# The last two blocks of an expert kernel: second-layer products alternated, adds per 128 tokens, state rows stored in three transfers

## The chip, the cores and the metric

The kernel runs on one core of one Trainium2 chip. The metric is the time on the device in microseconds; for each kernel it is the median of several executions. One more execution is recorded by the hardware profiler, and all views shown here come from it. In them PE is the matmul engine, PEld its weight loads, DVE the vector engine, ACT the scalar engine, and SP the engine that issues most of the stores. hps, A, E and Bseed are tiles in the matmul engine's accumulation memory (PSUM), a bank each: 128 partitions by 512 numbers of 32 bits.

## The reference

An attention between tokens and a small state comes first, and then a mixture of eight experts with a balanced routing. Cut to what matters:

```python
# attention: x (8, 8, 512, 64), state (8, 8, 32, 64), for each batch and head
xread = softmax(scale * x @ state.T) @ state
sread = softmax(scale * state @ x.T) @ x
rows = concat([xread, sread], axis=2)          # 512 + 32 rows per batch
x = rows.transpose(0, 2, 1, 3).reshape(8 * 544, 512)

# routing: P = exp(x @ w_gate), then 8 rounds of row and column normalisation
for e in range(8):
    h = np.maximum(x @ w1[e], 0.0)             # first layer: 512 -> 1024
    ye = h @ w2[e]                             # second layer: 1024 -> 512
    out += P[:, e:e + 1] * ye
```

The result has 4352 rows of 512 numbers: for each of the 8 batches 512 rows of tokens and then 32 rows of state.

## The kernel before

**Blocks.** The 4352 rows are worked on in nine blocks: blocks 0 to 7 are the 512 token rows of a batch each, and block 8 is the 8 x 32 = 256 state rows of all batches together. Expert 0 is done together with the attention, in an order that a planner at build time makes out of costs and due times (`issue`). Experts 1 to 7 follow in a plain loop (line 918) over the list `work`, expert after expert and block after block; that loop and the two functions that it steps are all that the change touches, and the order there is the order in which the program is written out.

**First layer** (`layer1`, line 246). For each of eight groups of 128 hidden units: matmuls into one of four `hps` banks (line 239; two matmuls of 512 columns for a token block, four of 256 for the state block), and a ReLU on ACT into the tile `Hm` (line 258). After each four groups, DVE makes four sums and differences of quarters of `Hm` (lines 264 to 267) into `sm` and `Hm`. `Hm` and `sm` come from the pool `hidden`, which holds two of each.

**Second layer** (`layer2`, line 270). The rows of a block are taken as two halves ("row 0" and "row 1"), the hidden units as two halves and the output columns as two halves of 256 (`DH`). The 2 x 2 x 2 product of these is made with seven products instead of eight, from the sums in `sm` and differences of weights in `T`. A product has `nk` parts of 128 tokens, two in a token block and one in the state block, and a part is four matmuls of 256 columns (line 285). Both parts of a product lie in the same bank. There are three banks per block: `A`, `E` and one of the two lasting `Bseed` tiles, which are used in turn. After the first product, ACT copies `A` into `Bseed` (line 310), on which later products accumulate:

```python
product(A, h(0, 0), w2h[:, :NJ, :DH], True)
nc.scalar.copy(out=Bb[:, :nk], in_=A[:, :nk])
product(Eb, s(0), T[:, 0], True);  add(Eb, 1, 1)
product(Bb, s(1), T[:, 1]);        add(Bb, 0, 1)
product(A, h(1, 0), w2h[:, NJ:, :DH]); add(A, 0, 0)
product(Bb, h(0, 1), T[:, 2]);     add(Bb, 1, 1)
product(Eb, s(2), w2h[:, NJ:, DH:]); add(Eb, 0, 1)
product(Bb, h(1, 1), T[:, 3]);     add(Bb, 1, 0)
```

`add(src, row, col)` is a DVE instruction for each 128 tokens (line 299): it takes 256 columns from the bank, multiplies them by the token's weight in `Pmat` and adds them into `acc`, the 4352 x 512 result in on-chip memory. All parts of a product are made before its adds are written out.

**Order.** Both layers are generators. Each step of the loop takes one product of the current block's second layer and then some groups of the next block's first layer, (0, 0, 1, 2, 2, 2, 1) of them after the seven products and the rest behind. So PE alternates between the two layers, with the second layer of one block beside the first layer of the next. For the very last block, block 8 of expert 7, there is no next block.

**Stores.** In expert 7, after a block's last product, SP issues the block's stores: for a token block four of 128 rows (256 KB, line 332), for the state block eight of 32 rows (64 KB, line 335), one for each batch.

Of the kernel before, what the change touches and what calls it, by code (L numbers as in the profile page):

```python
# [9 lines left out]
FP32 = mybir.dt.float32  # L10
FP16 = mybir.dt.float16
AX_X = mybir.AxisListType.X
ALU = mybir.AluOpType
# [74 lines left out]
def kernel(  # L88
# [9 lines left out]
    nc = tc.nc  # L98

    B, H, S, D = x.shape  # L100
    Ns = state.shape[2]
    Dm, E = moe_w_gate.shape
    F = moe_w1.shape[2]
    SB = S + Ns
# [8 lines left out]
    NJ = NFB // 2  # L113
    DH = Dm // 2
# [13 lines left out]
    def bank(shape, dtype, name, tag="bank"):  # L128
        return pools[tag].tile(shape, dtype, name=name, tag=tag)
# [3 lines left out]
    acc = persist.tile([128, NTB, Dm], FP32, name="acc")  # L133
# [15 lines left out]
    w2r = moe_w2.rearrange("e (fb p) d -> e p fb d", p=128)  # L149

    outx = [out[b * SB:b * SB + S, :].rearrange("(p sc) d -> p sc d", sc=NSC) for b in range(B)]
    outs = [out[b * SB + S:(b + 1) * SB, :] for b in range(B)]

    mw = ctx.enter_context(tc.tile_pool(name="moe_w", bufs=2))
    gsb = ctx.enter_context(tc.tile_pool(name="gate_sb", bufs=2))
# [85 lines left out]
    vt = {}  # L241
    ring = ["bank"]
    hid = {}
    seeds = []

    def layer1(e, bi):

        t0, tn = blocks[bi]
        th = tn // 2
        Hm = hpool.tile([128, 2, NJ, S], FP16, name="Hm", tag="Hm")  # L250
        sm = hpool.tile([128, 3, NJ, S // 2], FP16, name="sm", tag="sm")
        hid[(e, bi)] = (Hm, sm)
        for j in range(NJ):
            for i in range(2):
                fb = i * NJ + j
                hps = bank([128, S], FP32, "hps", "h")
                hidden_ps(e, bi, fb, hps[:, :tn])
                nc.scalar.activation(out=Hm[:, i, j, :tn], in_=hps[:, :tn], func=AF.Relu)  # L258
                if j % 2 and i:
                    jj = ds(j - 1, 2)  # L260
                    a11, a21 = Hm[:, 0, jj, :th], Hm[:, 0, jj, th:tn]
                    a12, a22 = Hm[:, 1, jj, :th], Hm[:, 1, jj, th:tn]
                    s1, s2, s4 = (sm[:, k, jj, :th] for k in range(3))
                    nc.vector.tensor_add(s1, a21, a22)  # L264
                    nc.vector.tensor_sub(a21, a11, a21)  # L265
                    nc.vector.tensor_sub(s2, s1, a11)  # L266
                    nc.vector.tensor_sub(s4, a12, s2)  # L267
                yield

    def layer2(e, bi, n):  # L270
        t0, tn = blocks[bi]
        nk = tn // 256
        th = tn // 2
        Hm, sm = hid.pop((e, bi))
        w2h, T = w16[e][1], tsum[e]
        tb = t0 // 128
        p = Pmat[:, :, e:e + 1]
        A = bank([128, 2, DH], FP32, "A", "A")
        Eb = bank([128, 2, DH], FP32, "E", "E")
        Bb = seeds[n % 2]  # L280

        def product(dst, lhs, rhs, first=False):
            for c in range(nk):
                for j in range(NJ):
                    nc.tensor.matmul(dst[:, c], lhs(j, c), rhs[:, j],  # L285
                                     start=first and c == 0 and j == 0, stop=(j == NJ - 1),
                                     skip_group_check=True)

        def h(i, half):
            return lambda j, c: Hm[:, i, j, ds(half * th + c * 128, 128)]  # L290

        def s(k):
            return lambda j, c: sm[:, k, j, ds(c * 128, 128)]

        def add(src, row, col):
            for c in range(nk):
                k = tb + row * nk + c
                dst = acc[:, k, ds(col * DH, DH)]
                nc.vector.scalar_tensor_tensor(out=dst, in0=src[:, c], scalar=p[:, k], in1=dst,  # L299
                                               op0=ALU.mult, op1=ALU.add)  # L300

        if e == 1:
            for k in range(tb, tb + 2 * nk):
                if k % 2:
                    nc.scalar.mul(acc[:, k, :], acc[:, k, :], Pmat[:, k, 0:1])
                else:
                    nc.vector.tensor_scalar(out=acc[:, k, :], in0=acc[:, k, :],
                                            scalar1=Pmat[:, k, 0:1], scalar2=None, op0=ALU.mult)
        product(A, h(0, 0), w2h[:, :NJ, :DH], True)
        nc.scalar.copy(out=Bb[:, :nk], in_=A[:, :nk])  # L310
        yield
        product(Eb, s(0), T[:, 0], True)
        add(Eb, 1, 1)
        yield
        product(Bb, s(1), T[:, 1])
        add(Bb, 0, 1)
        yield
        product(A, h(1, 0), w2h[:, NJ:, :DH])
        add(A, 0, 0)
        yield  # L320
        product(Bb, h(0, 1), T[:, 2])
        add(Bb, 1, 1)
        yield
        product(Eb, s(2), w2h[:, NJ:, DH:])
        add(Eb, 0, 1)
        yield
        product(Bb, h(1, 1), T[:, 3])
        add(Bb, 1, 0)
        if e == E - 1:
            for k in range(2 * nk):  # L330
                if bi < B:
                    nc.sync.dma_start(out=outx[bi][:, k, :], in_=acc[:, tb + k, :])
                else:
                    for i in range(128 // Ns):
                        nc.sync.dma_start(out=outs[k * (128 // Ns) + i],
                                          in_=acc[ds(i * Ns, Ns), tb + k, :])
        yield


# [43 lines left out]
    for q in range(NQ):  # L383
        for par in range(2):
            nc.gpsimd.tensor_copy(
                out=pick[:, q, par].rearrange("p (a i n) -> p a i n", i=2, n=Ns)[:, :, par ^ q],
                in_=identh.rearrange("p (a i n) -> p a i n", i=2, n=Ns)[:, :, par])
# [3 lines left out]
    for q in range(NQ):  # L391
        def load(q=q):
# [4 lines left out]
                           lambda eng, q=q: copy(eng, st16[:, q], st_st.tile.rearrange("p (q b d) -> p q b d", q=NQ, b=B)[:, q]),  # L397
                           [dma((0, q), 300, load, [], [] if q else [st_st])], [], [st_st]))
    wgd = dma((0, 2), 16, lambda: nc.sync.dma_start(
        out=wg_st, in_=moe_w_gate.rearrange("(kc p) e -> p kc e", p=128)))  # L400
# [32 lines left out]
    for b in range(B):  # L433
        for g in range(2):
# [13 lines left out]
            d = dma((0 if b < 1 else 3.2 if b < 2 else due_x(2 * b - 2), b, 0), 512, load, takes=[st])  # L448
# [249 lines left out]
    def tile_of(tag, shape):  # L698
# [3 lines left out]
    c = sk({"DVE": (0.36, 0.48)}, lambda: nc.vector.reduce_max(  # L702
        out=tile_of("lmx", [128, 1]), in_=logits.rearrange("p t e -> p (t e)"), axis=AX_X), gates)
    mT = psum([1, 128], FP32, "mT_ps")
    c = sk({"PE": (0.11, 0.35)}, lambda: nc.tensor.transpose(mT.tile, sm_["lmx"], ident32), [c], takes=[mT])
    c = sk({"DVE": (0.25, 0.40)}, lambda: nc.vector.tensor_reduce(
        out=tile_of("gm", [1, 1]), in_=mT.tile, op=ALU.max, axis=AX_X, negate=True), [c], uses=[mT])
    gb = psum([128, 1], FP32, "gm_ps")
    c = sk({"PE": (0.18, 0.45)}, lambda: nc.tensor.matmul(gb.tile, ones128[0:1, :], sm_["gm"]), [c], takes=[gb])
    c = sk({"DVE": (0.12, 0.25)}, lambda: nc.vector.tensor_copy(out=tile_of("nm", [128, 1]), in_=gb.tile),  # L710
           [c], uses=[gb])
    c = sk({"ACT": (0.40, 0.60)}, lambda: nc.scalar.activation(
        out=Pmat, in_=logits, func=AF.Exp, bias=sm_["nm"]), [c])
    for it in range(8):
# [10 lines left out]
        def colnorm(csb=csb):  # L725
# [7 lines left out]
        c = sk({"DVE": (2.10, 2.25)}, rownorm, [c])  # L733
        c = sk({"PE": (0.25, 0.60)}, lambda csb=csb: nc.tensor.matmul(csb.tile, ones128, sm_["cpart"]),
               [c], takes=[csb])
        c = sk({"DVE": (0.75, 0.90)}, colnorm, [c], uses=[csb])
# [50 lines left out]
    for bi in range(len(blocks)):  # L787
        t0, tn = blocks[bi]
# [5 lines left out]
        for fb in range(NFB):  # L794
            ps = psum([128, 512], FP32, "hps")
            h = slot(mh, 10, [128, 512], FP16, "hT")
# [10 lines left out]
        for tk in range(tn // 128):  # L807
            yps = psum([128, Dm], FP32, "yps")
            last = None
            for half in range(2):  # L810
                def mul(_, tk=tk, half=half, yps=yps, hT=hT):
                    w2h = wslots[0][1].tile
                    for fb in range(half * NJ, half * NJ + NJ):
# [4 lines left out]
                last = op((due_e(bi) + 13.5 * (0.4 + 0.075 * (2 * tk + half)),), {"PE": (0.87, 1.04)}, mul,  # L818
                          [h_ready[fb] for fb in fbs] + w2_ready(0)[2 * half:2 * half + 2] + [last],
                          [] if half else [yps], [hT[fb] for fb in fbs] + ([yps] if half else []))  # L820
# [32 lines left out]
    for bi in range(2):  # L853
        t0, tn = blocks[bi]
        th = tn // 2
# [50 lines left out]
    n = 0  # L906
# [8 lines left out]
                wload.pop(0)  # L915

    work = [(e, bi) for e in range(1, E) for bi in range(len(blocks))]
    for i, (e, bi) in enumerate(work):
        if bi == 1 and e + 1 < E:
            wload.append(load_w(e + 1, (nc.scalar,)))  # L920
        l2 = layer2(e, bi, i)
        l1 = layer1(*work[i + 1]) if i + 1 < len(work) and work[i + 1] not in hid else iter(())
        for k in range(7):
            next(l2)
            step()
            if k == 0 and i + 2 < len(work) and work[i + 2] not in vt:
                project(*work[i + 2])
            for _ in range((0, 0, 1, 2, 2, 2, 1)[k]):
                next(l1, None)
                step()  # L930
        for part in (l1, l2):
            for _ in part:
                pass
        if bi == len(blocks) - 3:
            for _ in (x for w in wload for x in w):
                pass
            wload.clear()


# [28 lines left out]
```

## Time and profile before

| | us |
|---|---|
| median of 3 runs | 782.14 |
| lowest and highest of them | 781.5 and 782.41 |
| profiled execution, its own time | 783.01 |
| span of the profile, from the first to the last instruction | 781.2 |
| PE busy in the span | 755.6 (97%) |
| DVE busy | 635.9 (81%) |
| ACT busy | 518.6 (66%) |
| last matmul ends | 775.2 |
| last add ends | 775.7 |

The profiled execution is 0.9 us above the median, and 1.8 us of it lie outside the span. A row of the chain in order of time gives a start, a duration and what the chain goes through there; a piece called "issue" is the time in which the next engine has not yet begun. A row of the timeline gives start, duration, engine, line, operation, what is written from what, how many instructions are merged, and in brackets the idle time ahead and what ended it. A row for stretches of time gives for each engine its busy time and, in brackets, the instructions that begin there, then the clock granted to PE, the share of the DMA engines, and GB/s.

### The profile page before, as it was taken

Reading aid. Unit: us, or ns where it says so; the run is one execution under the profiler, and the core shown is the slowest. Engines: PE = TensorE matmul, PEld = TensorE weight load, DVE = VectorE, ACT = ScalarE, POOL = GpSimd, SP = SyncE. Lnnn points to the kernel's source line nnn. Section 1 sums busy time; section 2 is a strip of 40 time slices with the busy share of each in tenths; the row PEclk is TensorE's granted clock in tenths of the full one; section 3 lists DMA queues with packets and bytes.
Section 4 is the critical chain, followed back from the end, with each engine's and each line's share of the span. In section 5 each row is a group of like instructions: output and inputs, shape, how many; then the busy total and the mean of one; then the engine's idle time right before and its main releaser. Section 6 shows DMA issues by size and latency. Waiting matters only on the chain.

```text
span 781.2 us, 16249 instructions
## 1 busy us (share of the span) xinstructions
PE 755.6 (97%) x6497; PEld 507.7 (65%) x6497; DVE 635.9 (81%) x1572; ACT 518.6 (66%) x1011; POOL 61.3 (8%) x114
## 2 busy tenths in 40 slices
PE   4799999999999999999999999999999999999996
PEld 3355444566667767766677667766667666766675
DVE  5788878968997888778887888878887888878885
ACT  5676766757767766676666666676657666576662
POOL 3546110010001000000001000000001000000000
PEclk9999999999999999999999999999999999999999
DMA  9996300060006000150006000060005100012223
GB/s 282 304 224 114 50 1 1 1 109 1 1 1 109 2 1 2 16 94 2 1 1 102 9 1 1 3 107 3 1 1 86 25 1 1 2 53 91 91 100 127
DMA packets 43772, 41.43 MB, mean 53 GB/s; under 512 B 18864, under 2 KB 34224, under 8 KB 43696
## 3 DMA queue, kind: packets, MB, share of 16 engines
q0 software_dynamic: 11200, 14.68, 11.6%
q1 hardware_dynamic: 31456, 25.45, 11.4%
q8 instruction: 51, 0.84, 0.5%
q10 hardware_dynamic: 1040, 0.26, 0.2%
q14 instruction: 25, 0.20, 0.1%
HBM read 42.48 MB, written 8.91 MB: 66 GB/s over the span
## 4 chain that ended last, share of the span: by engine, by line
PE 67%; DVE 3%; ACT 1%; issue 0%
PE hps L239 24%; PE Bseed L285 17%; PE E L285 12%; PE A L285 11%; PE v_ps L224 3%; DVE acc L299 1%; DVE sm L264 1%; ACT Hm L258 1%; DVE Hm L265 0%; DVE sm L267 0%; DVE sm L266 0%; DVE T L182 0%; ACT Bseed L310 0%
## 5 line engine op out<-in xcount | busy, mean ns | idle before, releaser
L258 ACT ACTIVATE Hm<-hps 128x512 f16<-128x512 f32 (+1 forms) x488 | 261.6, 572 | 181.8 <-PE hps L239 166.7
L285 PEld LDWEIGHTS <-Hm 128*128 128x128 f16 x1904 | 186.3, 98 | 69.2 <-issue 1.4
L239 PE MATMUL hps<-aT,V 128*128 128x512 f16 x864 | 230.5, 379 | 0.0
L299 DVE SCALAR_TENSOR_TENSOR acc<-Bseed,Pmat,acc 128x256 f32<-128x256 f32 x357 | 156.9, 479 | 56.9 <-PE Bseed L285 54.0
L285 PEld LDWEIGHTS <-sm 128*128 128x128 f16 x1428 | 134.4, 98 | 53.1 <-DVE sm L264 24.4
L285 PE MATMUL Bseed<-T,Hm 128*128 128x256 f16 x952 | 124.5, 273 | 0.7 <-DVE acc L299 0.4
L285 PE MATMUL A<-w2h,Hm 128*128 128x256 f16 x952 | 124.5, 273 | 0.0
L239 PEld LDWEIGHTS <-V 128*128 128x128 f16 x864 | 84.5, 98 | 44.4
L299 DVE SCALAR_TENSOR_TENSOR acc<-E,Pmat,acc 128x256 f32<-128x256 f32 x238 | 104.3, 477 | 9.2 <-PE E L285 5.3
L228 ACT CAST V<-v_ps 128x512 f16<-128x512 f32 x216 | 111.2, 609 | 0.0
L814 PE MATMUL yps<-w2h,hT 128*128 128x512 f16 x272 | 67.3, 383 | 0.0
L285 PE MATMUL E<-T,sm 128*128 128x256 f16 x476 | 64.4, 274 | 0.7
L264 DVE TENSOR_TENSOR sm<-Hm 128x512 f16<-128x512 f16 (+1 forms) x122 | 49.8, 408 | 18.6 <-ACT Hm L258 17.8
L299 DVE SCALAR_TENSOR_TENSOR acc<-A,Pmat,acc 128x256 f32<-128x256 f32 x119 | 52.4, 479 | 15.4 <-PE A L285 15.3
L285 PE MATMUL Bseed<-T,sm 128*128 128x256 f16 x476 | 62.3, 273 | 0.4 <-ACT Bseed L310 0.4
L285 PE MATMUL E<-w2h,sm 128*128 128x256 f16 x476 | 62.3, 273 | 0.0
L265 DVE TENSOR_TENSOR Hm<-Hm 128x512 f16<-128x512 f16 (+1 forms) x122 | 50.0, 410 | 4.2
L267 DVE TENSOR_TENSOR sm<-Hm,sm 128x512 f16<-128x512 f16 (+1 forms) x122 | 50.0, 409 | 4.2
L266 DVE TENSOR_TENSOR sm<-sm,Hm 128x512 f16<-128x512 f16 (+1 forms) x122 | 49.1, 402 | 0.0
L310 ACT COPY Bseed<-A 128x512 f32<-128x512 f32 (+1 forms) x63 | 34.5, 548 | 19.9 <-PE A L285 19.3
L164 POOL DMA_DIRECT2D w1h<-in_moe_w_dram x12 | 8.5, 713 | 457.8 <-PE hps L239 406.4
L814 PEld LDWEIGHTS <-hT 128*128 128x128 f16 x272 | 24.4, 99 | 27.0 <-issue 4.0
(117 smaller groups left out, 589.5 us busy)
## 6 DMA issues: line engine op xcount, KB each, us to landing
stage<-in_x_dram SPq DMA_DIRECT2D x16, 512.0 KB, 6.0
out_dram<-acc SPq DMA_DIRECT2D x32, 256.0 KB, 3.0
w1h<-in_moe_w_dram POOLq DMA_DIRECT2D x14, 512.0 KB, 5.8
w2h<-in_moe_w_dram POOLq DMA_DIRECT2D x14, 512.0 KB, 7.8
stage<-in_moe_w_dram SPq DMA_DIRECT2D x8, 512.0 KB, 5.7
out_dram<-acc SPq DMA_DIRECT2D x8, 64.0 KB, 1.7
stage<-in_state_dram ACTq DMA_DIRECT2D x1, 256.0 KB, 4.9
stage<-in_state_dram SPq DMA_DIRECT2D x1, 256.0 KB, 4.6
```

The lines of the kernel that those rows point to most:

```text
L224: nc.tensor.matmul(ps[q][ds(j * Ns, Ns), :], bdT[ds(r, 64), bi, q, ds(j * Ns, Ns)], w1h[ds(r, 64), 2 * q + j // 2, cols], tile_position=(r ...
L228: nc.scalar.copy(out=V[:, q, cols], in_=ps[q])
L239: nc.tensor.matmul(out, lhs, rhs, start=(k == 0), stop=(k == len(terms) - 1))
L258: nc.scalar.activation(out=Hm[:, i, j, :tn], in_=hps[:, :tn], func=AF.Relu)
L264: nc.vector.tensor_add(s1, a21, a22)
L265: nc.vector.tensor_sub(a21, a11, a21)
L266: nc.vector.tensor_sub(s2, s1, a11)
L267: nc.vector.tensor_sub(s4, a12, s2)
L285: nc.tensor.matmul(dst[:, c], lhs(j, c), rhs[:, j], start=first and c == 0 and j == 0, stop=(j == NJ - 1), skip_group_check=True)
L299: nc.vector.scalar_tensor_tensor(out=dst, in0=src[:, c], scalar=p[:, k], in1=dst, op0=ALU.mult, op1=ALU.add)
L310: nc.scalar.copy(out=Bb[:, :nk], in_=A[:, :nk])
L814: nc.tensor.matmul(yps.tile, hT[fb].tile[:, ds(tk * 128, 128)], w2h[:, fb, :], start=(fb == 0), stop=(fb == NFB - 1))
```

## The change

The last two entries of `work`, blocks 7 and 8 of expert 7, are taken out of the loop. Both their first layers are done during the second layer of block 6, with 0, 2, 3, 3, 3, 3, 2 groups after its seven products. The hidden units of block 8 get tiles of their own, `Hl` and `sl`, from a new pool. Then the two second layers are stepped in turn: two products of block 7, then one of block 8 and one of block 7 alternately, then the last two of block 8. Block 8 takes its `A` and `E` tiles from the four `hps` banks. In block 7 (`split=True`) each 128 tokens' add is written out directly behind their four matmuls, ahead of the matmuls of the next 128 tokens.

The stores of expert 7 are split by row: row 0 leaves after the sixth product, row 1 after the seventh. For token blocks they are the same transfers, on SP. The state block is stored by ACT in three transfers, each over four batches: columns 256 to 511 of row 1 (128 KB) after the fifth product, row 0 whole (256 KB) after the sixth, and columns 0 to 255 of row 1 (128 KB) after the seventh.

```diff
-    outs = [out[b * SB + S:(b + 1) * SB, :] for b in range(B)]
+    outs = out.rearrange("(b s) d -> b s d", b=B)
...
-        Hm = hpool.tile([128, 2, NJ, S], FP16, name="Hm", tag="Hm")
-        sm = hpool.tile([128, 3, NJ, S // 2], FP16, name="sm", tag="sm")
+        if (e, bi) == work[-1]:
+            Hm = lpool.tile([128, 2, NJ, tn], FP16, name="Hl")
+            sm = lpool.tile([128, 3, NJ, th], FP16, name="sl")
+        else:
+            Hm = hpool.tile([128, 2, NJ, S], FP16, name="Hm", tag="Hm")
+            sm = hpool.tile([128, 3, NJ, S // 2], FP16, name="sm", tag="sm")
...
-    def layer2(e, bi, n):
+    def layer2(e, bi, n, AE=("A", "E"), split=False):
...
-        A = bank([128, 2, DH], FP32, "A", "A")
-        Eb = bank([128, 2, DH], FP32, "E", "E")
+        A = bank([128, 2, DH], FP32, "A", AE[0])
+        Eb = bank([128, 2, DH], FP32, "E", AE[1])
...
+        def product(dst, lhs, rhs, row, col, first=False):
+            for c in range(nk):
+                mul(dst, lhs, rhs, c, first)
+                if split:
+                    add(dst, row, col, c)
+            for c in range(0 if split else nk):
+                add(dst, row, col, c)
+
+        def store(row, cols=slice(0, Dm)):
+            for c in range(nk if e == E - 1 else 0):
+                k = row * nk + c
+                if bi < B:
+                    nc.sync.dma_start(out=outx[bi][:, k, :], in_=acc[:, tb + k, :])
+                else:
+                    nc.scalar.dma_start(out=outs[ds(k * (128 // Ns), 128 // Ns), S:, cols],
+                                        in_=acc[:, tb + k, cols])
...
+        product(Bb, h(0, 1), T[:, 2], 1, 1)
+        if bi == B:
+            store(1, ds(DH, DH))
         yield
-        product(Eb, s(2), w2h[:, NJ:, DH:])
-        add(Eb, 0, 1)
+        product(Eb, s(2), w2h[:, NJ:, DH:], 0, 1)
+        store(0)
         yield
-        product(Bb, h(1, 1), T[:, 3])
-        add(Bb, 1, 0)
-        if e == E - 1:
-            for k in range(2 * nk):
-                if bi < B:
-                    nc.sync.dma_start(out=outx[bi][:, k, :], in_=acc[:, tb + k, :])
-                else:
-                    for i in range(128 // Ns):
-                        nc.sync.dma_start(out=outs[k * (128 // Ns) + i],
-                                          in_=acc[ds(i * Ns, Ns), tb + k, :])
+        product(Bb, h(1, 1), T[:, 3], 1, 0)
+        store(1, ds(0, DH))
         yield
...
-    for i, (e, bi) in enumerate(work):
+    lpool = ctx.enter_context(tc.tile_pool(name="last", bufs=1))
+    for i, (e, bi) in enumerate(work[:-2]):
...
+        slots = (0, 0, 1, 2, 2, 2, 1)
+        if i == len(work) - 3:
+            l1 = (x for w in work[-2:] for x in layer1(*w))
+            slots = (0, 2, 3, 3, 3, 3, 2)
...
+    i = len(work) - 2
+    p = layer2(*work[i], i, split=True)
+    q = layer2(*work[i + 1], i + 1, ("h", "h"))
+    for part in (p, p, q, p, q, p, q, p, q, p, q, p, q, q):
+        next(part)
```

More of the change, by code (lines that the diff above doesn't have):

```diff
@@ L277, in layer2, with mul @@
         p = Pmat[:, :, e:e + 1]
-        A = bank([128, 2, DH], FP32, "A", "A")
-        Eb = bank([128, 2, DH], FP32, "E", "E")
+        A = bank([128, 2, DH], FP32, "A", AE[0])
+        Eb = bank([128, 2, DH], FP32, "E", AE[1])
         Bb = seeds[n % 2]
[L282 to L287, printed above, removed]
+        def mul(dst, lhs, rhs, c, first=False):
+            for j in range(NJ):
+                nc.tensor.matmul(dst[:, c], lhs(j, c), rhs[:, j],
+                                 start=first and c == 0 and j == 0, stop=(j == NJ - 1),
+                                 skip_group_check=True)
         def h(i, half):
@@ L293, in s, with add @@
             return lambda j, c: sm[:, k, j, ds(c * 128, 128)]
-        def add(src, row, col):
-            for c in range(nk):
[L297 to L300, printed above, removed]
+        def add(src, row, col, c):
+            k = tb + row * nk + c
+            dst = acc[:, k, ds(col * DH, DH)]
+            nc.vector.scalar_tensor_tensor(out=dst, in0=src[:, c], scalar=p[:, k], in1=dst,
+                                           op0=ALU.mult, op1=ALU.add)
+        def product(dst, lhs, rhs, row, col, first=False):
+            for c in range(nk):
+                mul(dst, lhs, rhs, c, first)
[11 more added lines that the diff above has]
+                                        in_=acc[:, tb + k, cols])
         if e == 1:
@@ L308, in layer2 @@
                                             scalar1=Pmat[:, k, 0:1], scalar2=None, op0=ALU.mult)
-        product(A, h(0, 0), w2h[:, :NJ, :DH], True)
+        for c in range(nk):
+            mul(A, h(0, 0), w2h[:, :NJ, :DH], c, True)
         nc.scalar.copy(out=Bb[:, :nk], in_=A[:, :nk])
         yield
-        product(Eb, s(0), T[:, 0], True)
-        add(Eb, 1, 1)
+        product(Eb, s(0), T[:, 0], 1, 1, True)
         yield
-        product(Bb, s(1), T[:, 1])
-        add(Bb, 0, 1)
+        product(Bb, s(1), T[:, 1], 0, 1)
         yield
-        product(A, h(1, 0), w2h[:, NJ:, :DH])
-        add(A, 0, 0)
+        product(A, h(1, 0), w2h[:, NJ:, :DH], 0, 0)
         yield
-        product(Bb, h(0, 1), T[:, 2])
-        add(Bb, 1, 1)
+        product(Bb, h(0, 1), T[:, 2], 1, 1)
+        if bi == B:
+            store(1, ds(DH, DH))
         yield
-        product(Eb, s(2), w2h[:, NJ:, DH:])
-        add(Eb, 0, 1)
+        product(Eb, s(2), w2h[:, NJ:, DH:], 0, 1)
+        store(0)
         yield
-        product(Bb, h(1, 1), T[:, 3])
-        add(Bb, 1, 0)
-        if e == E - 1:
-            for k in range(2 * nk):
-                if bi < B:
-                    nc.sync.dma_start(out=outx[bi][:, k, :], in_=acc[:, tb + k, :])
-                else:
-                    for i in range(128 // Ns):
-                        nc.sync.dma_start(out=outs[k * (128 // Ns) + i],
-                                          in_=acc[ds(i * Ns, Ns), tb + k, :])
+        product(Bb, h(1, 1), T[:, 3], 1, 0)
+        store(1, ds(0, DH))
         yield
@@ L921 @@
         l2 = layer2(e, bi, i)
-        l1 = layer1(*work[i + 1]) if i + 1 < len(work) and work[i + 1] not in hid else iter(())
+        l1 = layer1(*work[i + 1]) if work[i + 1] not in hid else iter(())
+        slots = (0, 0, 1, 2, 2, 2, 1)
+        if i == len(work) - 3:
+            l1 = (x for w in work[-2:] for x in layer1(*w))
+            slots = (0, 2, 3, 3, 3, 3, 2)
         for k in range(7):
@@ L925 @@
             step()
-            if k == 0 and i + 2 < len(work) and work[i + 2] not in vt:
+            if k == 0 and work[i + 2] not in vt:
                 project(*work[i + 2])
-            for _ in range((0, 0, 1, 2, 2, 2, 1)[k]):
+            for _ in range(slots[k]):
                 next(l1, None)
```

## The prediction

> **What bounds the kernel now.** I read the page's chain first. 67% of the span is PE itself, so the middle of the kernel has nothing to give except PE work, and the change leaves all matmuls as they are. What can move is the end, so the next view is the chain in order of time, from the seam into the last block.
>
> ```profile
> 768.78 0.87 PE hps L239 x8
> 769.65 0.89 PE Bseed L285 x8
> ...
> 771.44 0.28 DVE sm L264
> ...
> 772.88 0.48 DVE acc L299
> 773.36 0.04 issue
> 773.40 0.61 PE Bseed L285 x4
> 774.01 0.03 issue
> 774.04 0.49 DVE acc L299
> 774.53 0.04 issue
> 774.58 0.61 PE Bseed L285 x4
> 775.19 0.03 issue
> 775.21 0.48 DVE acc L299
> ```
>
> Two prices are here. Eight matmuls in full flow take 0.87 us, so four take 0.435. But four matmuls, the add that reads them and the return to PE take 0.61 + 0.03 + 0.49 + 0.04 = 1.17 us. The last block alternates in just this way, because with 128 tokens per row each product has only four matmuls and the next product into the same bank waits for its add.
>
> The third view is the timeline of the end, the fourth the landing of the two kinds of stores (line 332, 256 KB each; line 335, 64 KB each), the fifth the DMA view of one block's four 256 KB stores.
>
> ```profile
> 774.99 3.62 SPq L335 DMA_DIRECT2D out_dram<-acc  x8
> 775.21 0.48 DVE L299 SCALAR_TENSOR_TENSOR acc<-Bseed,Pmat,acc 128x256 f32<-128x256 f32 x1 [0.25 <-PE Bseed L285]
> ```
>
> ```profile
> L332 SPq DMA_DIRECT2D out_dram<-acc x32: 332/373/1349, 699.5 to 771.5; - x32
> DMA to landing us min/median/max: 2.2/3.0/5.0
> ```
>
> ```profile
> L335 SPq DMA_DIRECT2D out_dram<-acc x8: 345/418/426, 775.0 to 778.2; - x8
> DMA to landing us min/median/max: 1.6/1.7/1.7
> ```
>
> ```profile
> GB/s 0 0 0 0 0 0 0 0 0 0 0 72 379 389 379 348 430 358 359 410 358 369 400 358 328 266 41 0 0 0 0 0 0 0 0 41 0 0 0 0
> ```
>
> The last add ends at 775.69, yet the span ends at 781.2. Between them SP issues eight 64 KB stores one after the other, 0.46 us apart, the last at 778.2; it lands 1.7 later, at 779.9, and 1.3 us of closing waits and barrier follow. So the end is bound first by PE and DVE taking turns, then by SP's issuing.
>
> **What the change takes away.** PE's idle time from the point where the order changes (753.3). At the seam 761.14 to 763.10 the chain takes 1.96 us for 16 matmuls of PE work, 1.74: 0.22 lost. From 769.65 to 775.19 it takes 5.54 us for 8 + 4 + 28 matmuls, 4.37 us without pauses: 1.17 lost. In sum 1.39; without it PE would end at 775.19 - 1.39 = 773.80. The change removes both losses: by then the first layers and their sums are done ahead, and each block's product stands between the other's. The denser stretch ahead of it, 16 first-layer products inside one block's second layer, has 13.1 us of PE work against ACT's 8 x 0.54 + 8 x 0.44 + 0.57 = 8.4 and some 11 of DVE; four hps banks let ACT lag by more than three products in a row. I cost it at nothing; if the cover failed, one missed bank would cost about one ACTIVATE, 0.5 us.
>
> The eight SP issues (3.62 us) become three on ACT's queue, two of them before the last add.
>
> **What the change adds: six stops.** Block 7's second layer now adds after each 128 tokens. Both 128-token halves of a product lie in one PSUM bank, and in the changed program the fifth matmul, first of the second half, waits for VectorE. The counts say for what: for the add of the first half, just issued. That is so in all six products of block 7 that have an add:
>
> ```
> Matmult E<-w2h,sm 128x256  (x4, first half)
> TensorScalarPtr acc<-E     (add of the first half, waits PE)
> Matmult E<-w2h,sm 128x256  [waits DVE]  (second half)
> ```
>
> PE takes its matmuls in order, so nothing gets past the waiting one: block 8's product is queued behind the second half and covers the second add, not the first. No trace of before shows a bank written in one half while the other is read; the bounds are nothing (the second half runs on) and the full turn above. The turn is the same pair of instructions on the same engines, and the wait is in the program, so I take the turn: 1.17 - 0.435 = 0.735 us a stop, 4.41 for six. DVE has no backlog that would add to it: a round has 8 + 4 matmuls and one stop, 0.435 + 0.87 + 0.735 = 2.04 us, and three adds at 0.40 to 0.48. Only the first stop is longer: block 8's last four sums (about 1.07 us after an ACTIVATE that ends near 765.07) stand on DVE ahead of it until about 766.17 instead of 766.00: 0.17.
>
> The Trainium skill ("PSUM — Partial Sum Buffer", section "PSUM bank collisions raise a hardware error") has a rule against adding by halves: PE writing and VectorE reading one bank at once is an error even at different columns, and the hardware does not hold one of them back. By it the sum has the full turn six times and no cheaper form of this edit exists within one bank; no run here shows a collision.
>
> PE then ends at 773.80 + 4.41 + 0.17 = 778.38, and the last add at 778.38 + 0.03 + 0.48 = 778.89, 3.20 us later than before.
>
> **The stores after that.** Before the last add ends, block 7's second row-1 store (256 KB, SP) is issued at about 778.08, and block 8's row-0 store (256 KB, ACT) at 778.5. The last 128 KB go out at 778.95, ahead of which the ACT queue is free (0.42 us an issue; ACT computes nothing then, so nobody waits behind it). From 64 KB in 1.65 and 256 KB in 2.2 us follows about 1.5 us fixed and 0.7 per 256 KB, which the DMA view confirms at 360 to 400 GB/s. The three overlap: 640 KB from 778.08 + 1.5 take 1.75, to 781.3, and 0.1 for the shorter 1 KB runs: 781.4. If they did not hinder each other it would be 778.95 + 1.85 = 780.8. Against 779.9 before, that is 1.5 later (0.9 to 2.1, the upper end with 1 KB runs at the price of 2 KB ones and an ACT issue at SP's slow 0.715). The close was 1.3 us; the counter of the last store is now the fourth of eight that SP looks at, not the first, so 1.1 to 1.3: I take 1.2. Block 7's row-0 stores and those of earlier blocks leave one product earlier, under PE work: nothing.
>
> The sum against the profiled span: 781.4 + 1.2 = 782.6, +1.4 us. The profiled execution took 783.01, of which 781.2 are span; it lies 0.87 over the median 782.14. So 784.4 for such a run, and **783.5** for the median, 0.17% slower. A bare 0.2% is 1.56 us, about what a measurement here can tell from no change.
>
> **Rivals.**
> *The halves run on (faster).* If the stops cost nothing, PE ends at 773.8 and the stores bind: from block 7's first row-0 store, issued near 771.75, 1.5 MB stream from 773.25 for 4.2 us, to 777.5, and with 1.2 the span is 778.7, -2.5: 779.6. Each 0.1 us off a stop gives 0.6; the kernel breaks even at stops of 0.5 and is 0.2% faster below 0.25. For it speaks that the before pays less for turns in wide blocks (one Bseed wait of 0.3 in the last 20 us); against it, the wait stands in the program and has nothing to hide under. 5%.
>
> *The store tail is longer (slower).* 1.5 MB leave in the last 7 us over two queues, and ACT's queue has last been used at the start of the kernel, where its one load took 4.9 us to land against SP's 4.6. In the block with the worst landings a 256 KB store took 5.0 instead of 2.2. If the last stores land 0.6 to 1.3 later than my 781.4, the time is 784.1 to 784.8. It decides from 0.2 us on, because 783.7 is the 0.2% line. For it: any delay behind the last add goes in full to the end. Against: no loads run then. 15%.
>
> *PE's clock falls (slower).* A stretch with PE busy 0.71 of 3.45 us was followed by 3.41 us at half clock:
>
> ```profile
> 28.40:31.80 3.40, 2.74 (x18) 1.15 (x16) 3.12 (x8) 3.16 (x7) 3.40 (x9) 1.00 1.09 347
> 31.80:35.25 3.45, 0.71 (x21) 0.72 (x22) 2.46 (x6) 1.21 (x5) 3.45 (x9) 1.00 1.19 245
> 35.25:38.66 3.41, 3.41 (x30) 1.67 (x26) 2.19 (x5) 1.26 (x5) 1.80 (x6) 0.50 1.11 340
> ```
>
> At half clock a round takes 1.305 more, so one such stretch costs 3.41 x 1.305 / 3.35 = 1.3 us and two 2.7: 784.8 to 786.2. Against it: in the new end PE works 1.305 of each 2.04 us, and at 25.0 to 28.4 it was busy 2.21 of 3.40, the same share, and kept the full clock afterwards. 5%. The Trainium skill ("TensorE: Matmul & The Clock Gate", section "A second HAM failure mode: psum-queue depth-cycling") says that pauses between groups of matmuls can throw the clock back; the row just given does not show it at this share.
>
> *The sum is right but milder:* stores don't hinder each other and the time is 782.8 or below; it is the lower end of the likeliest case, and 3% more go to it as unchanged.
>
> **Chances and range.** The likeliest case, six full stops with the stores as summed, has 72% and its own range 782.6 to 784.3; the line at 783.7 cuts it, with 47 of the 72 below. Faster: 5. Same: 47 + 3 = 50. Slower: 25 + 15 + 5 = 45. The range 782.4 to 784.9 takes in the likeliest case and nearly all of the long store tail, and leaves out the faster rival and most of the clock's.
>
> **What would show it.** Right: from about 766 on, six waits of PE for "DVE acc" at about 0.7 us each; the last add about 3 us later than 775.69; one 128 KB store from ACT right behind it; no idle PE at the two seams; the granted clock 1.00 to the end. Wrong: PE's last matmul ends before 776 (no stops), the span's end lies less than 3.0 or more than 4.5 us behind the last add (3.7 by the sum), or PE waits on ACT in the stretch 754 to 765.

## The result, and the profile after

The changed kernel took 789.60 us (median of 6 executions) against 782.27 for the kernel before: a ratio of 1.0091, 95% interval 1.0076 to 1.0106. It is slower by 7.3 us; the prediction said 1.4.

First the part that was foreseen. In the chain in order of time, these are two of block 7's products in the new end:

```profile
769.42 0.04 issue
769.46 0.61 PE Bseed L288 x4
770.07 0.02 issue
770.09 1.37 DVE acc L301 x3
771.46 0.04 issue
771.50 0.61 PE A L288 x4
```

From the second half at 769.46 to the next second half at 771.50 are 2.04 us, and in each such round PE stands still once. The view of who waited for whom, from 764 to 780, has the six stops (total, times, longest):

```profile
PE Bseed L288 <- DVE acc L301: 1.8, 3, 0.6
PE E L288 <- DVE acc L301: 1.3, 2, 0.7
PE A L288 <- DVE acc L301: 0.6, 1, 0.6
```

They sum to 3.7 us. The rest of a stop lies in PE's busy time: the first half's four matmuls take 0.60 us until the last one has ended (770.33 to 770.93 in the timeline), where in full flow the next would begin after 0.435. In six stops that is 1.0 us more.

The timeline shows where the rest went. The last add begins at 779.17 and ends at 779.65; the span ends at 789.3.

```profile
777.21 3.51 ACTq L318 DMA_DIRECT2D out_dram<-acc  x3
...
779.17 0.48 DVE L301 SCALAR_TENSOR_TENSOR acc<-Bseed,Pmat,acc 128x256 f32<-128x256 f32 x1
```

So 9.7 us follow the last add, where before it was 5.5 and the sum had 3.7. The three ACT stores were issued by 780.7. Each issue took 0.55 to 1.15 us, where SP's typical one for a 64 KB store before took 0.42:

```profile
L318 ACTq DMA_DIRECT2D out_dram<-acc x3: 552/817/1154, 777.2 to 779.9; - x3
```

The DMA view of 779 to 789 (slices of 0.25 us; the upper row is the mean busy share of the 16 DMA engines in tenths, the lower GB/s) shows the transfers:

```profile
DMA  4569999943250141013131222222221110000000
GB/s 127 139 160 352 373 402 401 352 180 90 66 25 25 25 41 25 33 57 66 66 74 74 98 98 106 98 98 94 90 78 70 70 61 29 25 8 0 0 0 0
```

From 779.75 to 781 SP's 256 KB stores of block 7 keep all engines busy at 350 to 400 GB/s. From 782 on, with nothing else to do, the state block's stores move at 25 to 106 GB/s, and the share stands at 2 tenths, about 4 engines of 16. The last one lands at 788.2. The trace also lists the landings that a store's engines report one by one: behind the one noted at the issue there are four for each of these three stores, spread over more than 1.5 us for the last two.

The start of a run varies by some microseconds, so kernels are compared from a common point, the last projection (the last matmul of line 224, at 742.16 in the profile before), all of whose work is the same. Beside e1 to e13 the kernel before was measured again, with medians of 782.50 to 782.69; their ratios, and what is said of them against before, go by these:

| kernel | to PE's last matmul | last add to end of span | projection to end | median | ratio to before (95%) |
|---|---|---|---|---|---|
| before | 33.02 | 5.54 | 39.08 | 782.27 | |
| changed | 36.31 | 9.66 | 46.49 | 789.60 | 1.0091 (1.0076 to 1.0106) |
| e1: one batch per transfer | 36.31 | 5.62 | 42.46 | 786.13 | 1.0047 (1.0032 to 1.0062) |
| e6: three stores on SP | 36.32 | 9.78 | 46.62 | 789.87 | 1.0096 (1.0078 to 1.0113) |
| e10: two batches per transfer | 36.32 | 13.95 | 50.79 | 794.37 | 1.0148 (1.0107 to 1.0189) |
| e2: the new stores alone | 33.02 | 9.34 | 42.88 | 787.08 | 1.0062 (1.0045 to 1.0080) |
| e3: no adds by halves | 31.64 | 11.01 | 43.47 | 787.50 | 1.0064 (1.0046 to 1.0081) |
| e8: by halves, two queues | 36.33 | 4.78 | 41.63 | 785.07 | 1.0031 (1.0014 to 1.0047) |
| e9: block 8 between halves, two queues | 33.67 | 6.67 | 40.86 | 783.36 | 1.0012 (0.9997 to 1.0027) |
| e5: no halves, two queues | 31.64 | 5.45 | 37.92 | 782.75 | 0.9996 (0.9979 to 1.0012) |
| e12: as e5, rows stored whole | 31.64 | 5.28 | 37.75 | 781.07 | 0.9985 (0.9976 to 0.9994) |
| e13: before, state stores on two queues | 33.02 | 4.09 | 37.63 | 780.59 | 0.9975 (0.9964 to 0.9986) |

The loss by the profile is 46.49 - 39.08 = 7.41 us: 3.29 up to PE's last matmul, and 4.12 behind the last add.

### The profile page after: what moved, and what is told of

The parts are those of the page before. It is cut to its first block, busy times and chain, and to the rows that moved or that the text cites. A ratio compares the mean times of both kernels' runs of the same rounds, so it can differ in the third digit from the quotient of the medians.

```text
span 789.3 us, 16246 instructions
## 1 busy us (share of the span) xinstructions
PE 755.7 (96%) x6497; PEld 508.3 (64%) x6497; DVE 636.2 (81%) x1572; ACT 518.7 (66%) x1011; POOL 61.5 (8%) x114
## 4 chain that ended last, share of the span: by engine, by line
PE 67%; DVE 3%; ACT 1%; issue 0%; DVEq 0%
PE hps L239 23%; PE Bseed L288 17%; PE E L288 12%; PE A L288 11%; PE v_ps L224 3%; DVE acc L301 2%; DVE sm L268 1%; ACT Hm L262 0%; DVE sm L271 0%; DVE Hm L269 0%; DVE sm L270 0%; DVE T L182 0%; ACT Bseed L330 0%; ACT Hl L262 0%; DVE sl L268 0%
## 5 line engine op out<-in xcount | busy, mean ns | idle before, releaser
L262 ACT ACTIVATE Hm<-hps 128x512 f16<-128x512 f32 (+1 forms) x480 | 258.4, 575 | 173.8 <-PE hps L239 158.8
```

## The experiments

**Shape or queue?** Two things were new about the stores: their shape (four batches of 32 rows in one transfer) and the queue that issues them (ACT). e1 changes only the shape, and with it the number of transfers.

```diff
-   nc.scalar.dma_start(out=outs[ds(k * (128 // Ns), 128 // Ns), S:, cols], in_=acc[:, tb + k, cols])
+   for i in range(128 // Ns):
+       nc.scalar.dma_start(out=outs[k * (128 // Ns) + i, S:, cols], in_=acc[ds(i * Ns, Ns), tb + k, cols])
```

> The changed kernel with each of the state block's three stores cut into four of 32 rows, one per batch, all still on ACT's queue; nothing else differs. Theory (shape): a store whose slowest dimension is 4 batches runs on 4 DMA engines and so takes several times as long; with 32 rows per transfer all engines work, each transfer lands 1.6 to 1.7 us after its issue as in the kernel before, and only the issuing of 12 transfers at about 0.46 us remains: the last add at 779.2, last issue near 782.5, landing 784.1, end 785.2 against 789.3, so about 785.5 us. Rival (queue): ACT's queue is slow after 780 us of rest, whatever the shape: the landings stay late and the time is 789 to 791.

It took 786.13: 3.5 us less, with four times the transfers. ACT's queue issues as quickly as SP's did before (0.43 us in the median against 0.42), and the stores land in 2.0 us against 1.7:

```profile
L319 ACTq DMA_DIRECT2D out_dram<-acc x12: 321/433/488, 775.9 to 781.3; - x12
...
DMA to landing us min/median/max: 1.5/2.0/3.3
```

e6 changes only the queue.

```diff
-   nc.scalar.dma_start(out=outs[ds(...), S:, cols], in_=acc[:, tb + k, cols])
+   nc.sync.dma_start(out=outs[ds(...), S:, cols], in_=acc[:, tb + k, cols])
```

> The changed kernel with the state block's three stores issued by SP and not by ACT; shape and order stay. Theory (shape): the stores still run on 4 engines, and the time stays within 1.5 us of the changed kernel's 789.6. Rival (queue): SP's queue is in use all along, the stores land 2 us after their issue, and the time is that of the prediction, 783.5.

It took 789.87, as the changed kernel, and its DMA view of 777 to 787 has the same long end at 2 tenths:

```profile
DMA  6899995323114101313122222222121000000000
```

The queue is cleared, the shape is what costs. e10 takes the other direction, two batches in a transfer.

```diff
+   for i in range(2):
+       nc.scalar.dma_start(out=outs[ds(k * (128 // Ns) + 2 * i, 2), S:, cols], in_=acc[ds(64 * i, 64), tb + k, cols])
```

> The changed kernel with each of the state block's three stores cut into two of 64 rows, two batches each, on ACT. Theory (a store runs on as many DMA engines as its slowest dimension, here 2): all 512 KB go through 2 engines, 256 KB each, 10.8 us at the 84 ns per 2 KB packet against 5.4 on 4 engines: the last landing 13 to 16 us behind the last add instead of 8.5, 795 to 797 us. Rival (fewer rows per store is what helps): between the four-batch form and the 32-row form, 787 to 788.

It took 794.37 (two executions), with 13.95 us from the last add to the end; the last store lands 13.0 us behind the last add, where the theory had 13 to 16. The time is just under what the shape theory asked for, and far from the rival. The trace lists two landings for each of these stores behind the one at the issue, and sixteen in all for each of e1's. The DMA view of 779 to 793 shows a share of 1 tenth and about 47 GB/s, half of the four-batch form's 95:

```profile
DMA  5963101111111111111201101011111111100000
GB/s 187 328 234 91 21 35 53 50 44 50 56 41 47 53 47 47 59 47 47 47 23 29 53 18 35 35 47 53 44 50 50 47 47 50 50 29 3 0 0 0
```

**The parts apart.** e2 has the order of before and the new stores; e3 has the new order and stores, but adds behind the whole product (`layer2(*work[i], i)` without `split=True`).

> The kernel before in its order of products and adds, with the changed kernel's stores alone (row 0 after the sixth product; the state block in three transfers on ACT). Theory (shape): 128 KB per DMA engine on 4 engines, 5.6 us from about 775.9, end 782.8 to 784.3 in the span, so 783.7 to 785.2 us, slower than before by 1.6 to 3. Rival (queue): the last store lands 8.3 us after its issue, as in the changed kernel: 786 to 787. If the stores were no loss at all, the saved issuing would give 780 to 781.

e2 took 787.08, worse than the theory's range: the new stores alone cost 4.4 us. The number is close to the one that the rival gave (786 to 787), but its cause is excluded by e6; the last of the three stores lands 8 us or more behind the last add in each form with four batches (8.2 here, 8.5 in the changed kernel, 9.9 in e3). The theory had only the number of engines; some 2 us of slow start come on top (see the last section).

> The changed kernel with the adds of block 7 behind the whole product, as before (no adds per 128 tokens); order and stores stay. Theory: PE's six stops of 0.7 us go, PE's last matmul and the last add come 4.4 us earlier; block 7's and the state block's stores then crowd the same 4 engines, so that 4.3 to 5.5 us of it reach the end: 784 to 785.3 us. Rival: the stops were hidden behind the store tail and the time stays at 788 to 790.

e3 took 787.50. PE's last matmul came 36.31 - 31.64 = 4.67 us earlier, as the theory had it, but only 2.1 of it (3.0 in the profile) reached the end; the other part was given back behind the last add (11.01 against 9.66). That the stores of both blocks crowded the same few engines is the likely reason, and was not isolated. Both the theory's time and the rival's were off; the truth lay between.

**The stops, with stores that use all engines.** e5, e8 and e9 store by batch, with ACT and SP in turn (`(nc.scalar, nc.sync)[i % 2].dma_start`). They differ only in block 7's products: whole, in halves, or in halves with block 8's product in between, where a step of `p` is half a product and its add (the loop alone is shown; `product` also stops after the first half's add):

```diff
-    for part in (p, p, q, p, q, p, q, p, q, p, q, p, q, q):
+    for part in (p,) + 6 * (p, q, p) + (q,):
```

> As the version with ACT and SP in turn, but with the adds per 128 tokens back in block 7. Theory (stops): six stops come back, PE's end is 4.6 to 4.7 us later and nothing hides it: 784 to 784.6. Rival: part of the 4.7 hides behind the stores: 782 to 783.

> As the version with adds per 128 tokens and two queues, but with block 8's product put between the two halves of block 7's product, not behind both. Theory (PE takes matmuls in order, and the stop is the turn from the first half's matmuls over its add and back, 1.17 us): the product of 0.435 fills a part, so each of the six stops shrinks from 0.735 to 0.30 and PE ends 2.6 us earlier than with the product behind: 781.5 to 782. Rival (PE's stop is a fixed price of splitting, wherever the other product is): as with the product behind, 784 to 784.6.

> The changed kernel without the adds per 128 tokens, and with each state store cut into four of 32 rows, one per batch, issued by ACT and SP in turn. Theory: PE ends 1.4 us earlier than in the kernel before (31.6 us after the last projection against 33.0), and behind the last add only two issues of 0.46 on each queue, a landing of 1.65 and a close of 1.1 remain, 3.7 in all against 5.5: faster than before by 2.5 to 3 us, 779.5 to 780. Rival: 1.5 MB of stores in the last 6 us fill the DMA engines and the end is set by bytes: about 1 us less gain, 780.5 to 781.

PE's last matmul answers cleanly: 36.33 in halves, 33.67 with block 8's product between (2.66 less; 2.6 was expected) and 31.64 without halves. In e9 the timeline shows the product that stands in the gap, block 8's four matmuls from `Hl` into Bseed, between the two halves of block 7's product into E:

```profile
770.21 0.60 PE L288 MATMUL E<-w2h,sm 128*128 128x256 f16 x4
770.65 0.60 PE L288 MATMUL Bseed<-T,Hl 128*128 128x256 f16 x4
770.85 0.48 DVE L301 SCALAR_TENSOR_TENSOR acc<-E,Pmat,acc 128x256 f32<-128x256 f32 x1
771.39 0.60 PE L288 MATMUL E<-w2h,sm 128*128 128x256 f16 x4
```

In full flow the second half would begin at 770.65 + 0.435 = 771.09; it begins at 771.39, a stop of 0.30 as expected.

The times answer less cleanly: 785.07, 783.36 and 782.75. Halves cost 2.3 us by the medians (3.7 by the profiles) and not the 4.67 that PE lost, and all three lie above what was expected, e5 above its rival's 780.5 to 781 too. The reason is behind the last add: the tail is 4.78 in e8, 5.45 in e5 and 6.67 in e9, where 3.7 was expected of e5. The landings are counted on eight counters, which the stores use in turn, so a store waits until the one eight places ahead has landed. In e5, SP needed 1.63 us for two issues, because the second waited for a store that was issued at 773.82 and landed at 776.48:

```profile
775.26 1.63 SPq L316 DMA_DIRECT2D out_dram<-acc  x2
777.14 1.78 SPq L319 DMA_DIRECT2D out_dram<-acc  x4
```

In e9 the new order of products also puts block 8's row-0 stores ahead of block 7's last two on SP's queue, and SP waits 0.8 us for a counter. These two 256 KB stores are issued 2.2 us behind the last add, which ends at 774.55:

```profile
776.72 0.84 SPq L318 DMA_DIRECT2D out_dram<-acc  x2
```

So e9's time is not that of the stops alone; PE's last matmul is what tells of them.

**Fewer transfers.** e12 drops the early half-row store and stores rows whole, so eight state transfers remain of twelve (`store(1)` after the seventh product).

> The order of the changed kernel without the adds per 128 tokens; the state block's rows are stored whole again, row 0 after its sixth and row 1 after its seventh product, each as four transfers of 32 rows by ACT and SP in turn (8 state transfers in place of 12). Theory (the 12 transfers with two queues lost their gain to the eight completion counters: a store waits until the one eight places ahead has landed): with 12 stores in all at the end, only the last two wait for a counter, so the last add at 32.5 us after the last projection is followed by 4 to 4.7 us and not 5.45, and the time is 1.5 to 2.5 us under before: 780 to 781. Rival (the bytes bind, not the counters): behind the last add again 5.4 us, and the time is that of before within 0.5 us.

781.07, ratio 0.9985 (0.9976 to 0.9994): faster than before by a little, just outside the theory's range; but its tail of 5.28 is the rival's 5.4. The run does not separate the two. SP's last two stores did wait for counters (total, times, longest):

```profile
SPq L319 <- DMA out_dram<-acc: 0.9, 2, 0.5
```

These counters were late because the state stores took 2.7 us (median) to land and not 1.7, while the DMA share stood at 8 to 9 tenths from 773.4 to 776.6. Some 1.5 MB leave within some 6 us in this order; that the bytes set the end of it was argued, not isolated.

**One edit to the kernel before.** e13 keeps the old order and issues the eight 64 KB state stores by ACT and SP in turn.

```diff
-   nc.sync.dma_start(out=outs[k * (128 // Ns) + i], in_=acc[ds(i * Ns, Ns), tb + k, :])
+   (nc.scalar, nc.sync)[i % 2].dma_start(out=outs[k * (128 // Ns) + i], in_=acc[ds(i * Ns, Ns), tb + k, :])
```

> The kernel before with one edit: its eight 64 KB state stores are issued by ACT and SP in turn and not all by SP. Theory (the end of before is bound by SP's eight issues at 0.46 us): four issues per queue, the last starts 0.5 us behind the last add and lands 1.65 later, so 3.5 to 3.7 us follow the last add in place of 5.54: faster by 1.8 to 2, 780.3 to 780.8. Rival (the transfers themselves bind, or ACT issues more slowly than SP): 781.5 to 782.5.

780.59, within the theory's range, ratio 0.9975 (0.9964 to 0.9986), the lowest median of all. The 3.62 us of issuing became two trains side by side:

```profile
773.95 1.75 SPq L335 DMA_DIRECT2D out_dram<-acc  x4
773.95 1.80 ACTq L335 DMA_DIRECT2D out_dram<-acc  x4
```

The tail fell from 5.54 to 4.09, not quite to the 3.6 expected: the stores now land in 2.1 (median), not 1.7, probably since two are under way at a time.

## Why the prediction was wrong, point by point

*What bounds the end before: right.* PE and DVE in turn, then SP's issues. e13 takes only the issuing apart and gains 1.9 us by the medians, 1.45 in the profiles (39.08 - 37.63); e3 shows that the reordering takes 33.02 - 31.64 = 1.38 us of idle PE away, where 1.39 was read from the chain.

*The denser stretch costs nothing: right.* With 31.64 in e3 there is no pause left that could belong to it, and e3's view of waits from 751 to 775 lists none of PE.

*Six stops: right in place, kind and size.* 4.41 + 0.17 = 4.58 was summed, 4.67 measured by taking the halves away. The last add, like PE's last matmul, came 3.29 later than before, where 3.20 was forecast. That the add between the halves makes the stop is shown by e3, and that the stop is a turn which other work can fill, and no fixed price, by e9. So "no cheaper form of this edit exists within one bank" was too strong: e9 stays within one bank and costs 33.67 - 31.64 = 2.03 us.

*The stores after the last add: wrong, and here the prediction fails.* The step is "640 KB from 778.08 + 1.5 take 1.75". It gave the state block's stores the rate of token stores, 360 to 400 GB/s, read from transfers of 128 rows that lie in one piece. The state stores go to four batches of 32 rows, and ran at up to about 100. By the same step the ACT issue was priced at 0.42 and measured at 0.55 to 1.15. The last landing was summed 2.5 us behind the last add (781.4 against 778.89) and came 8.5 behind it; the whole term, from the last add to the end of the span, was summed at 3.7 us and measured at 9.66. That is 6 us, and it is the whole miss (7.3 against 1.4). That the shape is the cause is shown by e1, e6 and e10; the slow first 2 us of the row-0 store are part of it, and why they are slow is open. The Trainium skill has the rule ("DMA: Bandwidth & Descriptors", section "Why a DMA increments its semaphore by 16 and not by 1"): a transfer runs on the largest number of engines, up to 16, that divides the slowest dimension on both of its sides. With 4 batches this gives 4 engines, with 2 it gives 2, with 32 rows 16; the traces agree, with four, two and sixteen landings per store and a share of 2 tenths and 1 tenth. The prediction did not weigh this rule.

*The rivals.* "The store tail is longer" named the right place with a 15% chance, but other causes (1.5 MB over two queues, and ACT's queue after a long rest; e6 excludes the second) and a quarter of the size. "PE's clock falls" did not happen: up to PE's end the granted clock was 1.00, with PE busy 1.42 of the 2.00 us from 775 to 777. "The halves run on" did not happen.

*What would show it wrong* was named rightly: the end of the span more than 4.5 us behind the last add.

## What to carry to other kernels

Before fewer, larger stores replace many small ones, look at the outermost dimension of each: at the end of a kernel, where a landing goes in full to the time, three stores in four pieces each cost 3.5 us more than twelve stores of one piece. An add put between two halves of one accumulator bank stopped the matmul engine for the full turn here; other work helped only where it was queued ahead of the second half. And take the smallest edit that answers the binding row first: here the chain ended in SP's issues, and sharing these between two queues won 1.9 us by the medians. With the stores on two queues as well, the reordering (e12, 37.75 from projection to end) was no better than the old order (e13, 37.63): its 1.4 us was lost again among the stores.

## What the runs showed of the hardware

- A store whose outermost dimension was 4 moved at some 95 GB/s, with 2 at some 47, while stores of 128 rows reached 350 to 400. Issuing one of four batches took 0.55 to 1.15 us on ACT (0.56 to 0.80 on SP in e6) against 0.32 to 0.49 for the transfers of 32 rows in e1.
- The row-0 store of four batches began at only 25 to 66 GB/s for some 2 us (781.5 to 783.9 in the changed kernel, and again in e6) before it came to 95. In those two it follows right behind SP's stores, but e2 has the same slow start, 27 to 48 GB/s from 776.3 to 778.1, more than 4 us after SP's last packet. So those stores are not needed for it. Why it is slow is open; no run isolated it.
- ACT's queue, unused for 770 us, issued its stores about as quickly as SP's (0.41 against 0.39 us in the median in e13) and landed them nearly as quickly (2.2 against 2.0 us).
